# The work behind the ramp as single steps, put in order per engine by a list scheduler in the source

## The chip, the core and the metric

The kernel runs on one core of a Trainium2 chip. A core has five engines with instruction queues of their own: PE (matrix products into PSUM), DVE (vector work), ACT (activations, copies, casts), POOL (vector work on SBUF only) and SP (here it only issues DMAs). Each engine takes its instructions strictly in the order in which the program lists them; semaphores make an instruction wait for results of other engines, and whatever stands behind it on the same engine waits too. PE writes to PSUM, of which this kernel uses eight banks. The metric is the device time of the program in microseconds (us). It is 724.07 us before the change, the median of three runs (723.14 to 725.74).

## The reference

The first half is retention attention over blocks of 64 positions with a decay per head, the second a gated feed-forward network on its normed output. Cut to what matters:

```python
for b in range(nb):                               # per head, 12 blocks
    intra = (q[b] @ k[b].T) * Dmask               # decayed scores in the block
    out[b] = intra @ v[b] + (q[b] * lam_pow) @ kv_state
    kv_state = lam_block * kv_state + (k[b] * rev_pow).T @ v[b]
x = out.transpose(...).reshape(3072, 512)         # tokens x model
xn = x / sqrt(mean(x * x, -1) + 1e-6) * rms_g
y = (silu(xn @ w_gate) * (xn @ w_val)) @ w_out    # 512 -> 1536 -> 512
```

## The kernel before

The 3072 tokens are six *groups* of 512 (`m`, 0 to 5), the 1536 hidden columns twelve *column blocks* of 128 (`f`, 0 to 11). One group times one column block is a *unit*: the gate and val products, the silu of the gate, the hidden product, and four output products that add to four PSUM accumulators (`acc`, tags po0 to po3). There are 72 units: group 0 blocks 0 to 5, group 1 all twelve, group 0 blocks 6 to 11, and then groups 2 to 5. Every operand of a product is split into a high and a low part, so that each product is three.

Attention of a group runs in four *pairs* of heads (class `Pair`). A pair is: `scores` (PE), decays on ACT, DVE and POOL, `state_sums` (PE) and `states` (DVE), `mix_chunks` and `mix_states` (PE), then `keep_output` and `keep_squares` (ACT) and `add_squares`. Group m + 1 is worked on during group m. Its norm (class `Norm`) then takes: the squares split in two (`split_squares`), one row-sum product, a first guess and three refinements of the inverse root on DVE (`seed`, `refine`: three steps each on 128x512), four scalings (`scaled_to`), sums of the scaled parts, and their splits (`high` on ACT, `low` on DVE, `low_sums` on POOL).

There are three stretches.

- **The ramp** (`ramp`, units 0 to 5): written out by hand, with the first groups' attention and the first weights. The change leaves it alone.
- **Ordinary units** (6 to 23): `unit` issues gate (twelve matmuls, bank `pg`), val (twelve, bank `pv`), the hidden product `mul` (L958), `high` (L969) and `low` (L976), and the output products of the unit before. In between stand the conversion of the remaining weights (`Weights.take`, `split`), column norms and scale factors for the later half-precision weights (`columns`, `column_norms`, `bounds`, `factors`; the last two are some twenty small DVE steps), pairs of group 2 (units 16 to 20), whose `pst` and `po` use the banks `pg` and `pv`, its norm (21 to 23), the halving of the output weights (`halve_o`), and the weight sums (`WeightSums`).
- **Units of seven products** (24 to 71): `unit_of_sums` computes gate and val by seven products of half the width (Winograd's form of Strassen's scheme), six matmuls of 128x256 each, from sums of weights and sums of inputs. Two banks a and b take turns: products 1, 6, 7, 4 go to a and 2, 5, 3 to b; `keep` (ACT, L933) copies a aside, `sum` (DVE, L936) adds b to the copy, `silu_half` (L940) and `mul_sums` (L945) follow. In odd units a and b are the tiles `pg` and `pv`; in even units they are the two halves of one tile, `pp` (L919), which attention's scores and the norm also use. PE's order is written out: 1, 2, something to fill, 6, filler, 5, 7, filler, 4, filler, 3. The fillers are the output products of the unit before last (`outs`) and the pieces of attention. Refinement and scaling of the norm are queued with a cost each (`Tasks`) and drawn at two places of a unit.

The weight sums of block f (`WeightSums`: two adds on POOL, four sums on DVE, three casts on ACT, three remainders on POOL) are needed by the products of block f. `SUMS` puts them at units 18, 19, 20 and 24 to 32, and `HALVE` the halvings at units 18 to 20 and 24 to 26. `unit` issues a unit's DVE sums first (L1346), ahead of that unit's own `mul` (L1368).

What sets the order is the order of the calls alone: the source runs under a manual schedule, and waits are derived per tile from the calls as they were issued.

## Time and profile before

| | us |
|---|---|
| median of the runs (3) | 724.07 |
| the profiled execution | 722.93 |
| its span, first to last instruction | 721.1 |
| mean granted clock of PE over the span | 0.981 |

The span leaves out what lies before the first and behind the last instruction, 1.8 us. All work runs on one core, so the end of the chain is the end of the run. "Busy" of PE counts the time in which at least one matmul is under way; a matmul lasts longer than the distance to the next, so they overlap. Idle time shown in brackets is that of the engine just before the instruction, with what ended it. The names of tiles are those of the program: `pp`, `pa`, `pb`, `pg`, `pv` are banks of gate and val, `po`, `pst`, `pa` with L479 those of attention, `tx` stands for the sums of inputs and for the copies and sums beside them, `ws` and `r` for weight sums, `hh` for the hidden values.

### The profile page before, as it was taken

How to read it: one execution, taken by the hardware profiler on the slowest of the kernel's cores; microseconds unless marked ns; L12 is line 12 of the kernel's file. 1: busy time of each engine (PE TensorE's matmuls, PEld its weight loads, DVE VectorE, ACT ScalarE, POOL GpSimd, SP SyncE). 2: the span in 40 equal slices, each digit the busy share in tenths (PEclk: the TensorE clock that was granted, in tenths of full speed). 3: DMA queues.
4: the chain of work that ended last, by engine and by line, in shares of the span. 5: the costliest groups of instructions: out<-in, count | busy, mean ns of one | idle time of the engine just before them, and what ended most of it. 6: DMA issues, size and time to landing. Idle time of an engine off the chain costs nothing.

```text
span 721.1 us, 12347 instructions
## 1 busy us (share of the span) xinstructions
PE 662.8 (92%) x5007; PEld 444.3 (62%) x5007; DVE 423.2 (59%) x799; ACT 329.1 (46%) x674; POOL 158.4 (22%) x144
## 2 busy tenths in 40 slices
PE   8999999999977788789978899998899998899997
PEld 8755755555643445566656676666577666666664
DVE  6899667776544585566666443376543467533333
ACT  4795557775254424444424443334443334433332
POOL 3101110011265415577621111001111000000000
PEclk9999999999999998999989999999999999999999
DMA  8956423430130002201100131100130000010001
GB/s 322 354 202 234 175 89 108 155 117 0 60 117 1 1 0 73 71 34 60 59 1 1 59 118 59 59 2 1 59 117 2 1 2 1 4 56 1 1 0 60
DMA packets 14313, 51.13 MB, mean 71 GB/s; under 512 B 1712, under 2 KB 1968, under 8 KB 12848
## 3 DMA queue, kind: packets, MB, share of 16 engines
q1 hardware_dynamic: 13968, 49.69, 19.3%
q8 instruction: 39, 0.64, 0.4%
q10 hardware_dynamic: 288, 0.66, 0.3%
q14 instruction: 18, 0.15, 0.1%
HBM read 44.05 MB, written 6.29 MB: 70 GB/s over the span
## 4 chain that ended last, share of the span: by engine, by line
PE 44%; DVE 9%; ACT 6%; POOL 3%; issue 2%; DVEq 0%; ACTq 0%
PE pp L890 14%; PE pa L890 7%; PE pb L890 5%; PE acc L758 5%; PE acc L759 4%; PE acc L760 4%; DVE tx L936 2%; ACT sg L940 2%; PE po L539 2%; POOL r L829 1%; DVE sg L945 1%; ACT tx L933 1%; PE pa L479 1%; PE po L550 1%; DVE ws L840 1%
## 5 line engine op out<-in xcount | busy, mean ns | idle before, releaser
L759 PE MATMUL acc<-wo,hh 128*128 128x512 f16 (+1 forms) x288 | 111.4, 387 | 0.0
L760 PE MATMUL acc<-wo,hh 128*128 128x512 f16 (+1 forms) x288 | 111.3, 386 | 0.0
L758 PE MATMUL acc<-wo,hh 128*128 128x512 f16 x216 | 83.3, 386 | 0.2 <-DVE hh L976 0.2
L890 PEld LDWEIGHTS <-wg 128*128 128x128 f16 x576 | 56.2, 98 | 42.7 <-issue 23.3
L890 PEld LDWEIGHTS <-wo 128*128 128x128 f16 x576 | 55.8, 98 | 38.3 <-issue 16.5
L933 ACT COPY tx<-pp 128x256 f32<-128x256 f32 x72 | 26.8, 372 | 108.6 <-PE pp L890 107.8
L739 PE MATMUL pv<-x,wv 128*128 128x512 f16 x288 | 68.5, 386 | 5.0 <-ACT sq L582 5.0
L739 PE MATMUL pg<-x,wg 128*128 128x512 f16 x288 | 68.6, 383 | 0.3 <-ACT x L688 0.3
L969 ACT CAST hh<-sg 128x512 f16<-128x512 f32 (+1 forms) x72 | 44.6, 619 | 53.0 <-DVE sg L958 35.4
L890 PEld LDWEIGHTS <-wv 128*128 128x128 f16 x576 | 57.4, 100 | 17.0 <-issue 9.2
L933 ACT COPY tx<-pa 128x256 f32<-128x256 f32 x72 | 26.8, 372 | 84.6 <-PE pa L890 84.6
L499 POOL TENSOR_TENSOR qkv<-qkv,pw 128x512 f32<-128x512 f32 x22 | 29.2, 1330 | 127.7 <-PE pa L479 122.6
L936 DVE TENSOR_TENSOR tx<-pp,tx 128x256 f32<-128x256 f32 x48 | 20.4, 424 | 62.7 <-PE pp L890 51.0
L890 PE MATMUL pp<-x,wg 128*128 128x256 f16 x288 | 39.8, 275 | 15.5 <-ACT sg L940 12.9
L739 PEld LDWEIGHTS <-wv 128*128 128x128 f16 x288 | 27.9, 99 | 40.0 <-issue 8.9
L890 PE MATMUL pp<-tx,wo 128*128 128x256 f16 x288 | 40.0, 275 | 11.6 <-DVE tx L936 11.6
L739 PEld LDWEIGHTS <-wg 128*128 128x128 f16 x288 | 26.6, 98 | 34.3 <-issue 5.4
L890 PE MATMUL pp<-x,wv 128*128 128x256 f16 x288 | 37.5, 278 | 9.5 <-ACT x L688 6.9
L976 DVE TENSOR_TENSOR hh<-sg,hh 128x512 f16<-128x512 f32 x54 | 39.5, 731 | 9.3 <-ACT hh L969 7.7
L945 DVE SCALAR_TENSOR_TENSOR sg<-tx,cv,sg 128x512 f32<-128x512 f32 x48 | 39.1, 815 | 5.2 <-ACT sg L940 2.2
L940 ACT ACTIVATE sg<-sg,cg 128x256 f32<-128x256 f32 x48 | 24.4, 509 | 36.8 <-DVE sg L936 36.8
L936 DVE TENSOR_TENSOR tx<-pb,tx 128x256 f32<-128x256 f32 x48 | 20.4, 424 | 32.3 <-PE pb L890 29.5
(189 smaller groups left out, 1230.4 us busy)
## 6 DMA issues: line engine op xcount, KB each, us to landing
qkv<-in_qkv_dram SPq DMA_DIRECT2D x47, 512.0 KB, 4.9
raw_gv<-in_weights_dram SPq DMA_DIRECT2D x11, 1024.0 KB, 6.6
raw_o<-in_weights_dram SPq DMA_DIRECT2D x12, 512.0 KB, 3.9
out_dram<-o SPq DMA_DIRECT2D x23, 256.0 KB, 2.1
partial<-in_weights_dram SPq DMA_DIRECT2D x2, 512.0 KB, 11.7
qkv<-in_qkv_dram ACTq DMA_DIRECT2D x1, 512.0 KB, 4.5
out_dram<-o SPq DMA_DIRECT2D x1, 128.0 KB, 2.1
out_dram<-o ACTq DMA_DIRECT2D x1, 128.0 KB, 1.9
```

Source lines behind the costliest of these rows:

```text
L499: eng.tensor_mul(self.qT, self.qT, pw[:, p : p + 1, :].broadcast_to([P, GC, P]))
L739: nc.tensor.matmul(ps, w[:, kk, :], x[:, kk, :], start=i == kk == 0, stop=i == 2 and kk == NK - 1,)
L758: nc.tensor.matmul(acc, hl[:, ts_], oh, start=first, stop=False)
L759: nc.tensor.matmul(acc, hh[:, ts_], ol, start=False, stop=False)
L760: nc.tensor.matmul(acc, hh[:, ts_], oh, start=False, stop=last)
L890: nc.tensor.matmul(ps, w(ow, k), x(ox, k), start=first and i == k == 0, stop=i == 2 and k == 1, skip_group_check=True,)
L933: nc.scalar.copy(self.kept[:, i], self.pa)
L936: nc.vector.tensor_add(out, self.pb, self.kept[:, i])
L940: nc.scalar.activation(self.sg[:, half], src, AF.Silu, scale=cg[:, self.f, 0:1])
L945: nc.vector.scalar_tensor_tensor(self.sg, self.val, cv[:, self.f : self.f + 1], self.sg, ALU.mult, ALU.mult)
L969: nc.scalar.copy(self.hh, self.sg)
L976: nc.vector.tensor_sub(self.hl, self.sg, hh)
```

## The change

`unit`, `unit_of_sums`, `Tasks` and their helpers go. Their work becomes a list of steps. Each has an engine, a cost in us, a place `at` counted in units, the things it reads and writes by name, and the buffers that it opens. `Plan.run` goes through a model of the engines: it starts a step when what it needs is done, plus 0.15 us (0.28 from PE to ACT or DVE) and when a buffer is free. Of the steps up to 1.3 units ahead, PE takes the one with the smallest `at` that is ready; the other engines take the smallest `at`, or a later one that fits in ahead of it with at most 0.2 us lost. The step with the earliest start is then issued, so the program's order is the order of modelled starts. A DVE step that starts while POOL is at work costs a quarter more in the model. Loads (LD, LO) and stores (ST) are engines of the model; all go to SP's queue.

Other differences:

- Helpers are cut into single steps: `halve_o` becomes `Halves`, `columns` becomes `Column`, `scores`, `states` and `mix_chunks` go by two chunks each, `WeightSums` by parts. The two remainder buffers of a halving come from `o` (three buffers, shared with the output tiles) and no longer from `raw_o`.
- Groups 2 and 3 (`QUICK`) get the norm of the ramp: row sums with one column, the power -0.5 on POOL for 128x4 values, and a spread by four products (`quick`, `mean`, `root`, `spread`); the split of squares, the guess and the nine refinement steps go for these two groups. Groups 4 and 5 keep them.
- Weight sums are placed at 18.6, 19.6, 20.3 and from 24.5 on one per unit; halvings at 18.35 to 22.35 for blocks 6 to 11 and at 24.5 to 28.5 for blocks 0 to 5.
- The copy out of the accumulators and the store are steps of their own (`out_rows`, `send`).

```diff
@@ -691,7 +719,10 @@
             eng.tensor_sub(self.xl[:, kk, :], self.xns.pop(kk), self.xh[:, kk, :])
 
         def scaled_to(self, kk):
-
+            if self.m in QUICK and kk == 0:
+                r = self.r
...
+
+        def first(self, u):
+            self.banks(u)
+            self.add(1)
+
+        def add(self, n):
+            Product(self.m, self.f).add(
+                n, self.pb if n in (2, 5, 3) else self.pa, n in (1, 2, 5)
+            )
...
+        def sum_val(self, t, i):
+            half = slice(t * HG, (t + 1) * HG)
+            nc.vector.tensor_add(self.val[:, half], self.pb, self.kept[:, i])
+
+        def sum_gate(self):
+            self.sg = tmp.tile([P, G], F32, tag="t", name=f"sg_{self.m}_{self.f}")
+            nc.vector.tensor_add(self.sg[:, HG:], self.pb, self.kept[:, 0])
...
+    class Plan:
+
+
+        LAG = {("PE", "PE"): 0.0, ("PE", "ACT"): 0.28, ("PE", "DVE"): 0.28}
+        ENGINES = ("PE", "ACT", "DVE", "POOL", "LD", "LO", "ST")
 
...
+        def add(self, eng, cost, at, fn, *args, r=(), w=(), new=(), lasts=0.0):
+            self.steps.append((eng, cost, at, fn, args, tuple(r), tuple(w), tuple(new), lasts))
+
...
+        def run(self, horizon=1.3, reach=420):
+            deps = self.links()
...
+                best = None
+                for eng, c in found.items():
+                    now = clock[eng]
+                    c = sorted(x for x in c if x[1] < 1e9)
+                    if not c:
+                        continue
+                    pick = None
+                    if eng == "PE":
+                        pick = next((x for x in c if x[1] <= now + 0.05), None)
+                        pick = pick or min(c, key=lambda x: x[1])
+                    else:
+                        limit = 1e9
+                        for x in c:
+                            start = max(now, x[1])
+                            if start + self.steps[x[2]][1] <= limit + 0.2:
+                                pick = x
+                                if x[1] <= now + 0.05:
+                                    break
+                            limit = min(limit, start)
+                    start = max(now, pick[1])
+                    if best is None or start < best[0]:
+                        best = start, eng, pick[2]
...
+                start, eng, i = best
+                _, cost, at, fn, args, r, w, new, lasts = self.steps[i]
+                if eng == "DVE" and start < pool_until:
+                    cost *= 1.25
+                if eng == "POOL":
+                    pool_until = start + cost
+                clock[eng] = start + cost
+                end[i] = start + cost + lasts
+                if eng == "PE":
+                    progress = max(progress, at)
...
+                order.append((start, cost, eng, at, fn, args))
+                left.remove(i)
                 fn(*args)
...
+    def halve_steps(f, at):
+        h = Halves(f)
+        place = {HALF: NF, 0: NF - 1}.get(f, f - 1)
+        step("ACT", 0.72, at, h.high, r=["ts", "cv"], w=[f"w16_{f}:o", f"wo_{f}"], new=[(f"w16_{f}", f"wo{place}")])
+        step("ACT", 0.72, at + 0.1, h.rest_low, r=[f"wo_{f}", "ts"], w=[f"rl{f}", f"rh{f}"],
+             new=[(f"rl{f}", "o"), (f"rh{f}", "o")])
+        step("DVE", 0.76, at + 0.1, h.rest_high, r=[f"wo_{f}", "ts", f"w16_{f}:o"], w=[f"rh{f}"])
+        step("POOL", 1.28, at + 0.2, h.low, r=[f"rl{f}", f"rh{f}"], w=[f"w16_{f}:o"])
...
+    def sum_steps(f, at):
+        s = WeightSums(f)
+        tag = "w" if f < 3 else "a"
...
+            step("POOL", 1.15, at + 0.1 * i, s.whole, i, tag, r=[f"w{'vg'[i]}{f}"], w=[f"r{f}:{i}"],
+                 new=[] if i else [(f"r{f}", tag)])
+        for i in range(2):
+            step("DVE", 0.84, at + 0.5 + 0.1 * i, s.sums, i, to, r=[f"r{f}:0", f"r{f}:1"], w=[f"ws{f}"],
+                 new=[] if i else [(f"ws{f}", to)])
+        places = (
+            [f"w16_{ORDER[f]}:s"], [f"third{f}", "cols" if f < HALF else "partial"], [f"wg{f}"]
+        )
+        costs = [(0.6, 1.15), (0.4, 0.67), (0.4, 0.67)]
+        for i, to in enumerate(places):
+            step("ACT", costs[i][0], at + 0.9 + 0.05 * i, s.high, i, r=[f"ws{f}"], w=to)
+            step("POOL", costs[i][1], at + 1.2 + 0.05 * i, s.low, i, r=[f"ws{f}"], w=to)
...
+    def out_steps(u, h, ats):
+        m, f = h.m, h.f
+        first = f == 0 or (m == 0 and f == HALF)
+        weights = f"w16_{f}:o" if h.half else f"wo_{f}"
+        for t, at in enumerate(ats):
+            r = [f"hh{u}", weights] + ([] if h.half else [f"hl{u}"])
+            step("PE", 0.65 if h.half else 0.7, at, h.out, t, r=r, w=[f"acc{m}_{t}"],
...
+    def pair_scores(q, at):
+        n = f"{q.m}_{q.p}"
+        for i in range(2):
+            step("PE", 0.6, at + 0.02 * i, q.scores, range(2 * i, 2 * i + 2), r=[f"q{n}:q", f"q{n}:K"],
+                 w=[f"pa{n}"], new=[] if i else [(f"pa{n}", "ps")])
+        for j in range(2):
+            step("ACT", 0.5, at + 0.1, q.decay_k, j, w=[f"q{n}:k"])
+        step("DVE", 1.22, at - 1, q.decay_a, r=[f"pa{n}"], w=[f"a{n}"], new=[(f"a{n}", "a")])
+        step("POOL", 1.3, at + 0.1, q.decay_q, w=[f"q{n}:q"])
...
+    def pair_mix(q, at):
+        n = f"{q.m}_{q.p}"
+        m, p = q.m, q.p
+        for i in range(2):
+            step("PE", 0.54, at + 0.01 * i, q.mix_chunks, range(2 * i, 2 * i + 2), r=[f"q{n}:v", f"a{n}"],
+                 w=[f"po{n}"],
+                 new=[] if i else [(f"po{n}", "pv")] + [(f"x{m}", f"xs{SLOT_OF[m]}")] * (p == 0))
+        step("PE", 0.87, at + 0.05, q.mix_states, r=[f"q{n}:q", f"state{p}"], w=[f"po{n}"])
+        step("ACT", 0.57, at - 1, q.keep_output, r=[f"po{n}"], w=[f"x{m}:h{p}", f"x{m}:l{p}"])
+        step("ACT", 0.59, at - 1, q.keep_squares, r=[f"po{n}"], w=[f"s{n}"],
+             new=[(f"s{n}", "t" if p else "sq")])
...
+        if m in QUICK:
+            root = f"pr{m}"
+            step("PE", 0.9, at + 0.1, quick, r=[f"s{m}_0"], w=[f"pss{m}"], new=[(f"pss{m}", "ps")])
+            step("DVE", 0.25, at - 1, n("mean"), r=[f"pss{m}"], w=[f"y{m}"])
+            step("POOL", 1.0, at - 1, n("root"), w=[f"y{m}"])
+            step("PE", 1.0, at + 0.2, n("spread"), r=[f"y{m}"], w=[root], new=[(root, "ps")])
+            at -= 1
...
+    def strassen(u, h):
+        m, f = h.m, h.f
+        a, b = f"pa{u}", f"pb{u}"
+        banks = [(a, "pg"), (b, "pv")]
...
+        g, v = f"wg{f}", f"wv{f}"
+        s12, s3 = f"w16_{ORDER[f]}:s", f"third{f}"
+        step("PE", cost, u, h.first, u, r=[v, *x01], w=[a], new=banks)
+        step("ACT", 0.37, u - 1, h.keep, 0, r=[a], w=["kept0:0"])
+        step("PE", cost, u + 0.05, h.add, 2, r=[v, *x23], w=[b])
+        step("DVE", 0.42, u - 1, h.sum_val, 0, 0, r=[b, "kept0:0"], w=["kept1:0"])
+        step("PE", cost, u + 0.25, h.add, 6, r=[s12, *t], w=[a])
+        step("ACT", 0.37, u - 1, h.keep, 1, r=[a], w=["kept0:1"])
+        step("PE", cost, u + 0.4, h.add, 5, r=[s12, *t], w=[b])
+        step("PE", cost, u + 0.45, h.add, 7, r=[s3, *t], w=[a])
+        step("ACT", 0.37, u - 1, h.keep, 0, r=[a], w=["kept0:0"])
+        step("DVE", 0.42, u - 1, h.sum_gate, r=[b, "kept0:0"], w=[f"sg{u}:1"], new=[(f"sg{u}", "t")])
+        step("ACT", 0.47, u - 1, h.silu_half, 1, r=[f"cg{f}"], w=[f"sg{u}:1"])
+        step("PE", cost, u + 0.75, h.add, 4, r=[g, *x01], w=[a])
+        step("ACT", 0.47, u - 1, h.silu_half, 0, r=[a, f"cg{f}", f"sg{u}:1"], w=[f"sg{u}:0"])
+        step("PE", cost, u + 0.8, h.add, 3, r=[g, *x23], w=[b])
+        step("DVE", 0.42, u - 1, h.sum_val, 1, 1, r=[b, "kept0:1"], w=["kept1:1"])
+        step("DVE", 0.78, u - 0.9, h.mul_sums, r=["kept1:0", "kept1:1", "cv"], w=[f"sg{u}:0", f"sg{u}:1"])
+        tag = ("hh", "hl")[f % 2]
+        both = [f"sg{u}:0", f"sg{u}:1"]
+        step("ACT", 0.62, u + 0.2, h.high, r=both, w=[f"hh{u}"], new=[(f"hh{u}", tag)])
+        step("DVE", 0.7, u + 0.3, h.low, r=both, w=[f"hh{u}"])
+
...
+    QUICK = (2, 3)
+    SUMS = [(18, 18.6), (19, 19.6), (20, 20.3)]
+    SUMS += [(2 * NF, 2 * NF + 0.5 + 1.0 * (f - 3)) for f in range(3, NF)]
...
+            if HALF <= u - 1 < 2 * NF:
+                late = 0.66 if u < 2 * NF else 0.2
+                out_steps(u - 1, hs[u - 1], [u + late + 0.03 * t for t in range(GC)])
+            if 2 * NF <= u - 2:
+                out_steps(u - 2, hs[u - 2], [u + t for t in (0.15, 0.35, 0.6, 0.65)])
+            if u >= end:
                 continue
-            h = Hidden(m, f)
-
...
+                for i, f in enumerate(ORDER):
+                    halve_steps(f, u + 0.35 + 0.8 * i if i < HALF else 2 * NF + 0.5 + 0.8 * f)
+            for f, v in enumerate(SUMS):
+                if v[0] == u:
+                    sum_steps(f, v[1])
```

822 lines of the change are left out of this document (466 added, 356 removed).

## The prediction

> **What bounds the kernel now.** I read the page first, then the busy time by stage, then the waits of PE, then the timeline of a few units.
>
> ```profile
> span 721.1 us, 12347 instructions
> ...
> PE 662.8 (92%) x5007; PEld 444.3 (62%) x5007; DVE 423.2 (59%) x799; ACT 329.1 (46%) x674; POOL 158.4 (22%) x144
> ```
>
> PE is busy 92% of the span and no other engine is above 59%. So the kernel is bound by PE, and the change can only win where PE stands still, or runs on a lower clock. The stages show where that is. I cut at unit 7 (97.81), at 200, at the first unit of seven products (unit 24, 268.33), and at the first units of groups 3, 4 and 5 (395.06, 506.62, 616.90).
>
> ```profile
> core 0: us, PE busy (x) PEld busy (x) DVE busy (x) ACT busy (x) POOL busy (x), PEclk, DMA share, GB/s
> 97.81:200.00 102.19, 102.19 (x589) 59.69 (x589) 72.11 (x147) 59.03 (x107) 14.95 (x17) 1.00 0.27 93
> 200.00:268.33 68.33, 56.70 (x334) 28.84 (x333) 35.92 (x61) 28.78 (x52) 31.26 (x28) 0.93 0.09 31
> 268.33:300.00 31.67, 22.95 (x189) 16.51 (x189) 21.29 (x40) 14.09 (x31) 18.80 (x16) 0.87 0.20 68
> 300.00:395.06 95.06, 85.95 (x679) 59.64 (x675) 60.33 (x108) 41.28 (x96) 47.04 (x42) 0.96 0.10 34
> 395.06:506.62 111.56, 103.24 (x876) 74.21 (x874) 58.40 (x110) 44.42 (x98) 13.76 (x10) 1.00 0.14 48
> 506.62:616.90 110.28, 102.97 (x876) 74.12 (x874) 58.07 (x106) 43.72 (x97) 11.39 (x8) 1.00 0.09 30
> 616.90:721.10 104.20, 93.65 (x674) 65.50 (x671) 39.41 (x70) 36.28 (x79) 1.64 (x1) 1.00 0.06 21
> ```
>
> Length less PE's busy time is PE's idle time: 0, 11.6, 8.7, 9.1, 8.3, 7.3 and 10.5 us, together 55.6. Up to 200 PE never stops at full clock; there the change can only lose. Between 200 and 395 the clock is below 1, which costs at most (1 - clock) x busy: 4.0 + 3.0 + 3.4 = 10.4 us.
>
> ```profile
> engine line waited for: us in total, times, longest us
> PE pp L890 <- ACT sg L940: 12.9, 16, 1.7
> PE pp L890 <- DVE tx L936: 11.6, 23, 1.5
> PE pp L890 <- ACT x L688: 6.9, 2, 3.5
> PE po L539 <- DVE sg L958: 5.9, 2, 3.7
> PE pv L739 <- ACT sq L582: 5.0, 3, 2.3
> ```
>
> Each row gives a total, a count and the longest. These waits come from the order of the instructions, not from a lack of engine time. In an ordinary unit with attention, `po` and `pv` take turns in one bank:
>
> ```profile
> 218.54 1.09 PE L539 MATMUL po<-a,qkv 128*64 128x128 f32 x16 [3.69 <-DVE sg L958]
> ```
>
> ```profile
> 215.10 1.47 DVE L840 TENSOR_TENSOR ws<-r 128x256 f32<-128x256 f32 x1 [7.19 <-POOL r L829]
> ...
> 217.74 0.74 DVE L958 SCALAR_TENSOR_TENSOR sg<-pv,cv,sg 128x512 f32<-128x512 f32 x1
> ```
>
> PE waits 3.69 us for the hidden product (L958) that frees the bank. DVE stood still for 7.19 us before it, in front of a weight sum that waits for POOL, and the hidden product was queued behind that sum. On PE the four output products of the previous unit are queued behind the waiting matmul. The waits on L688 are the norm of the next group, which arrives late at two starts of a group. The first two rows of the waits are mostly the even units:
>
> ```profile
> 664.71 1.47 PE L890 MATMUL pp<-x,wv 128*128 128x256 f16 x12
> ...
> 666.28 0.37 ACT L933 COPY tx<-pp 128x256 f32<-128x256 f32 x1 [1.55 <-PE pp L890]
> ...
> 666.68 0.42 DVE L936 TENSOR_TENSOR tx<-pp,tx 128x256 f32<-128x256 f32 x1 [0.49 <-ACT tx L933]
> 667.16 0.82 PE L890 MATMUL pp<-tx,wo 128*128 128x256 f16 x6 [0.33 <-DVE tx L936]
> ...
> 671.06 0.82 PE L890 MATMUL pp<-x,wg 128*128 128x256 f16 x6
> ...
> 671.92 0.47 ACT L940 ACTIVATE sg<-pp,cg 128x256 f32<-128x256 f32 x1 [0.52 <-PE pp L890]
> 672.44 0.81 PE L890 MATMUL pp<-x,wg 128*128 128x256 f16 x6 [0.56 <-ACT sg L940]
> ...
> 673.09 0.82 PE L890 MATMUL pa<-x,wv 128*128 128x256 f16 x6
> ...
> 673.75 0.82 PE L890 MATMUL pb<-x,wv 128*128 128x256 f16 x6
> ...
> 674.00 0.38 ACT L933 COPY tx<-pa 128x256 f32<-128x256 f32 x1 [1.61 <-PE pa L890]
> ```
>
> In an odd unit (673.09) the two banks are two tiles, `pa` and `pb`, and the first copy (674.00) starts 0.25 after product 2 has begun, when product 1 is through. In an even unit both banks are one tile, `pp`: the copy at 666.28 waits for product 2 although it reads only what product 1 wrote, product 6 at 667.16 waits for a DVE sum of the other bank, and product 3 at 672.44 for the silu of the other bank. So what is issued earlier against either half of `pp` holds back what comes later. Each such stop costs its idle time and about 0.17 more, because the matmuls overlap: the six at 671.06 stand 1.38 us ahead of the next six, where 0.66 does without a stop (673.09 to 673.75), so the stop is worth 0.72 and shows 0.56 idle.
>
> **The change part by part.** (a) *Group 5, units 60 to 71* (10.5 idle). Six even units lose 0.33 + 0.56, together 5.3. Product 3 is now placed right behind product 4, ahead of the silu in program order, so the 0.56 goes; the silu then waits for product 3 too, some 0.65 later, and two products of the next unit cover that. The 0.33 stays: the plan names the halves of `pp` as separate things and puts the sum ahead of product 6, so the false wait survives. The longest wait for the DVE sum, 1.5 in the waits above, is in unit 60, behind the last norm's steps; 1.2 of it goes. The rest is the tail: the chain sum, product, cast, remainder, last outputs and stores, which no order shortens.
>
> ```profile
> 714.42 0.39 PE L758 MATMUL acc<-wo,hh 128*128 128x512 f16 x1 [0.16 <-DVE hh L976]
> ```
>
> PE waits only 0.16 there; the 6.7 us from this row to the end of the span hold the last twelve matmuls, then copies and stores. Nothing is won there. Saved: 3.4 + 1.2 and 7 times 0.17, 5.8 us.
>
> (b) *Groups 3 and 4* (15.6 idle). The same stops in 12 even units, and norm steps of the next group that stand ahead of the sums and silus. In the eight even units with attention the state sums now come in addition to the output product ahead of product 6, and fill the 0.33. DVE is busy half the time (58.4 of 111.6), so single norm steps fit into its holes two units earlier. I leave 4.5 idle and add 4 for some 24 starts: 15 us saved.
>
> (c) *Group 2, 268 to 395* (17.8 idle, clock 6.4 at most, of which I take 5, and 4 for some 24 starts: 27). The new short chain removes nine refinement steps and two before them:
>
> ```profile
> L675 DVE SCALAR_TENSOR_TENSOR hy<-yt,hy 128x512 f32<-128x512 f32 x12 | 8.3, 691 | 0.3
> ...
> L671 DVE TENSOR_TENSOR yt<-hy 128x512 f32<-128x512 f32 x12 | 8.3, 690 | 0.3
> ```
>
> ```profile
> L637 PE MATMUL pr<-ident,y x16: 273/275/356, 26.0 to 86.2; 128*128 128x128 f32 x16
> L628 POOL TENSOR_TENSOR y<-ms,power x2: 1023/1025/1027, 24.5 to 83.1; 128x4 f32<-128x4 f32 x2
> ```
>
> That is 9 x 0.69 = 6.2 us of DVE less for each of groups 2 and 3, and one POOL power of 1.03 and eight small fp32 matmuls more. On PE these cost at most 8 x 0.275 = 2.2 us a group, if none overlaps the next, and no less than 0, since the row sums that go are fewer; attention's products of the same width overlap (sixteen in 1.09 at 218.54), so I take half, 1.1, and 2.2 for both groups. The weight sums move to one per unit from unit 24.5 and all six later halvings come there too:
>
> ```profile
> L829 POOL TENSOR_TENSOR r<-wv 128x512 f32<-128x512 f16 x12 | 17.4, 1453 | 1.1 <-DMA out_dram<-o 1.1
> ...
> L268 POOL TENSOR_TENSOR wo<-rest 128x512 f16<-128x512 f32 x12 | 15.8, 1316 | 18.2 <-DVE rest L265 18.2
> L829 POOL TENSOR_TENSOR r<-wg 128x512 f32<-128x512 f16 x12 | 15.2, 1268 | 0.0
> ...
> L857 POOL TENSOR_TENSOR wo<-ws,wo 128x512 f16<-128x512 f32 x12 | 13.9, 1160 | 31.9 <-ACT wo L852 28.9 <-DVE hy L663 3.0
> ```
>
> (The first two columns after the bar are the total and the mean, in ns, of one.) One weight sum takes 2.7 for the two adds, 1.2 for the widest remainder, and two of half its width, which I put at 0.8 (between 0.6 and 1.2): 5.5 us of POOL, where the plan reckons 4.8. With 66 us now in these 127 and three halvings more (4 us), POOL would be busy 70 of about 105 us: two thirds, with 2.5 units of lead before a sum is used. DVE falls from 81.6 to about 75 of 105. Both fit, but both are in strict order, so a late POOL result stops everything behind its reader on DVE, the sums that free PE's banks among it. The halvings also leave `raw_o` for two of the three `o` buffers, which group 0's last output tiles hold until they are stored; there a halving can wait for a store, and a POOL addition behind it. I leave 10 of the 27: 17 saved.
>
> (d) *Units 18 to 23, from 200* (11.6 idle, clock 4.0 of which I take 3, 1.4 for starts: 16). The hidden product is given a unit's lead over the halvings and weight sums that now stand before it on DVE, and output products fill PE's waits for a bank. The chain bounds, spread, factors of unit 18 stays on the path of its product; attention and the output, gate and val products lie beside it. Where that cover fails, the price is the 3.69 seen above. I leave 5: 11 saved.
>
> (e) Units 6 to 17: same order of gate, val, output. Nothing to win; 1 us lost somewhere is my estimate between 0 and 4. Stores and loads still share SP's queue; a store that waits for its copy holds loads back, but those are due units later and DMA is at most 0.27 busy: nothing. Cutting a helper into single steps, and scores, states and mixes into halves, adds no instruction: nothing.
>
> Sum: 5.8 + 15 + 17 + 11 - 2.2 - 1 = 45.6. The profiled execution took 722.93 us (1.8 around its span), the median of runs 724.07, 1.1 more. 722.93 - 45.6 + 1.1 = 678.4; I say **678**.
>
> The ends: with every stop closed but the tail I get 657, with (c) and (d) at nothing 706; both are worked out next.
>
> **Rivals.** *The heavy stages give nothing back* (c and d fail, a and b hold): 20.8 - 3.2 = 17.6, **706**. For it speaks that between 200 and 395 DVE and POOL feed each other all the time; against it, that neither is above two thirds busy on average.
>
> *Slower.* The order is fixed by reckoned times, to 0.1 us, without slack. Its weak place is DVE beside POOL:
>
> ```profile
> L945 DVE SCALAR_TENSOR_TENSOR sg<-tx,cv,sg x48: 750/752/1753, 286.1 to 712.2; 128x512 f32<-128x512 f32 x48
> ```
>
> ```profile
> L840 DVE TENSOR_TENSOR ws<-r x12: 409/426/1484, 192.1 to 362.3; 128x256 f32<-128x256 f32 x12
> ```
>
> One block lasts about 1.0 us (1753 - 752; 1484 - 426), where the plan adds a quarter, 0.2. If one such block reached PE in each of the 48 last units, 48 us would eat the gain of 45.6; from there the kernel is slower, and with 60 blocks it is **738**. Against it: the medians sit at the minimum, and after 395 POOL works only 27 us in all. The Trainium skill, in "SBUF — State Buffer", section "SBUF: two separate sides", states that the port pair which DVE and GpSimd share is an exclusive lock held for a whole instruction; the longest rows agree, the medians say that it is rarely met. As an estimate by that page: if each of group 2's twelve hidden products lost one block of 1.0, the sum would be 33.6 and the time 690.
>
> *Everything closes*: all idle but 4 of tail, 8 of clock and 9 of starts, less 2: 67, **657**. *Nothing changes*, because the old waits return elsewhere one for one: 724.
>
> **How the numbers follow.** Forecast (662 to 697) 0.66; heavy stages fail (697 to 718) 0.16; all closes (under 662) 0.06; no change 0.03; slower 0.09. What a measurement can tell is about 0.3%, 2.2 us, so: faster 0.88, same 0.03, slower 0.09. The range leaves out the outer part of each side: 658 to 708.
>
> **What would show it.** PE's waits for the silu before product 3 gone, about 0.33 before product 6 left in even units without attention; clock 1.00 between 200 and 395; no wait on the casts of the norm at a group's start; PE without idle time up to 200. Wrong would be: PE waiting in group 2 on DVE sums that stand behind a weight sum or a halving, or DVE rows well over 0.75 us.

## The result, and the profile after

The changed kernel takes 671.0 us (median of four runs, 670.44 to 672.56), the kernel before 724.85 us beside it (723.14 to 725.74). The ratio is 0.9263, with a 95% interval of 0.9238 to 0.9288: 53.9 us less, where 46 were forecast. The profiled run of the changed kernel took 672.56 us, the longest of the four.

First the page of the changed kernel: the span, the busy time by engine, and PE's granted clock in forty slices (in tenths, so 9 stands for 90% or more).

```profile
span 670.8 us, 12331 instructions
...
PE 652.3 (97%) x5035; PEld 442.9 (66%) x5035; DVE 428.0 (64%) x779; ACT 328.9 (49%) x672; POOL 160.1 (24%) x144
...
PEclk9999999999999999999999999999999999999999
```

PE is busy 97% of the span. Its busy time fell by 10.5 us although 28 more of its matmuls are on record: the mean granted clock went from 0.981 to 0.998, and 0.017 of 662.8 us is 11.3, of the same size. DVE has 20 instructions fewer and is busy 4.8 us longer. That is taken up at the end.

Then the busy time by stage, in the order PE, PEld, DVE, ACT, POOL, with the granted clock behind them. The cuts are the first products of units 7, 18, 24, 36, 48 and 60.

```profile
100.26:195.68 95.42, 95.42 (x513) 54.49 (x512) 63.98 (x129) 56.13 (x102) 14.37 (x16) 1.00 0.25 85
195.68:258.65 62.97, 62.09 (x422) 33.38 (x422) 45.77 (x71) 30.60 (x55) 35.28 (x29) 1.00 0.15 50
258.65:366.76 108.11, 101.70 (x874) 73.80 (x873) 85.80 (x139) 57.34 (x129) 67.06 (x58) 1.00 0.15 50
366.76:473.34 106.58, 105.93 (x916) 76.42 (x914) 59.49 (x109) 45.98 (x101) 12.59 (x9) 1.00 0.15 51
473.34:573.89 100.55, 99.89 (x847) 72.92 (x846) 56.40 (x105) 42.26 (x92) 11.22 (x8) 1.00 0.09 32
573.89:670.80 96.91, 90.15 (x661) 64.34 (x659) 37.42 (x68) 34.88 (x77) 0.00 (x0) 0.99 0.06 23
```

Length less busy time of PE is its idle time: 0, 0.9, 6.4, 0.7, 0.7 and 6.8 us, together 15.4 where it was 55.6. The last 6.8 are 4.4 behind the last matmul and eight short stops. What is left to win sits in units 24 to 35, with 6.4. Set against the same units before (from first product to first product; the first row begins with unit 6, at 92.61 before and 94.36 now):

| units | before, us | after, us | won | forecast |
|---|---|---|---|---|
| 6 to 17 | 99.24 | 101.32 | -2.1 | -1 |
| 18 to 23 | 76.48 | 62.97 | 13.5 | 11 - 1.1 |
| 24 to 35 (group 2) | 126.73 | 108.11 | 18.6 | 17 - 1.1 |
| 36 to 59 (groups 3, 4) | 221.84 | 207.13 | 14.7 | 15 |
| 60 to the end | 104.25 | 96.89 | 7.4 | 5.8 |
| sum | | | 52.1 | 45.6 |

The spans differ by 50.3, not 52.1, because the ramp's first gate product starts at 33.87 us in this profile and at 32.10 in that of before. The ramp is the same code in both.

The waits of PE after (engine, line, what it waited for: total in us, times, longest):

```profile
PE pp L939 <- DVE tx L990: 3.1, 10, 0.3
PE pp L939 <- DVE sg L994: 2.6, 5, 0.7
PE pp L939 <- ACT tx L986: 2.2, 4, 1.0
...
PE pp L939 <- DVE xn L731: 0.9, 1, 0.9
```

The rows of 12.9 (silu), 11.6 (sums), 6.9 (casts of the norm), 5.9 (`po`) and 5.0 (`pv`) are gone. What heads the list is 3.1 us in ten stops of a third of a microsecond. They are the even units. The timeline of unit 70, PE first, then DVE, shows one:

```profile
645.89 1.47 PE L939 MATMUL pp<-x,wv 128*128 128x256 f16 x12
...
648.34 0.81 PE L939 MATMUL pp<-tx,wo 128*128 128x256 f16 x6 [0.33 <-DVE tx L990]
...
652.24 1.47 PE L939 MATMUL pp<-x,wg 128*128 128x256 f16 x12
```

```profile
647.86 0.42 DVE L990 TENSOR_TENSOR tx<-pp,tx 128x256 f32<-128x256 f32 x1 [0.49 <-ACT tx L986]
```

Products 4 and 3 now stand as one row of twelve at 652.24: the stop between them is gone. Product 6 at 648.34 still waits 0.33 us for a sum (647.86) that reads the other half of `pp`. Even units without attention went from 8.38 to 7.66 us, odd ones stayed at 7.17.

### The profile page after: what moved, and what is told of

Same layout as the page of the kernel before. It is cut to its first block, busy times and chain, and to the rows that moved or that the text cites. A ratio compares the mean times of both kernels' runs of the same rounds, so it can differ in the third digit from the quotient of the medians.

```text
span 670.8 us, 12331 instructions
## 1 busy us (share of the span) xinstructions
PE 652.3 (97%) x5035; PEld 442.9 (66%) x5035; DVE 428.0 (64%) x779; ACT 328.9 (49%) x672; POOL 160.1 (24%) x144
## 4 chain that ended last, share of the span: by engine, by line
PE 86%; DVE 8%; ACT 2%; POOL 1%; issue 1%; DMA 0%; DVEq 0%; ACTq 0%; POOLq 0%
PE pp L939 16%; PE pv L758 9%; PE acc L777 9%; PE pg L758 9%; PE pa L939 8%; PE acc L779 8%; PE acc L778 8%; PE pb L939 6%; PE pa L508 4%; PE po L569 3%; PE po L580 2%; PE pst L537 2%; DVE tx L990 1%; DVE ws L887 1%; ACT tx L986 1%
## 5 line engine op out<-in xcount | busy, mean ns | idle before, releaser
L758 PE MATMUL pv<-x,wv 128*128 128x512 f16 x288 | 67.0, 379 | 0.0
L990 DVE TENSOR_TENSOR tx<-pp,tx 128x256 f32<-128x256 f32 x48 | 20.3, 423 | 51.7 <-ACT sg L998 40.0
L1035 DVE TENSOR_TENSOR hh<-sg,hh 128x512 f16<-128x512 f32 x54 | 43.2, 800 | 5.1 <-ACT hh L1028 4.2
L1004 DVE SCALAR_TENSOR_TENSOR sg<-tx,cv,sg 128x512 f32<-128x512 f32 x48 | 39.6, 825 | 4.1 <-DVE tx L990 0.5
L994 DVE TENSOR_TENSOR sg<-pp,tx 128x256 f32<-128x256 f32 x24 | 10.1, 423 | 45.5 <-ACT tx L986 43.5
L939 PE MATMUL pp<-x,wg 128*128 128x256 f16 x288 | 35.5, 272 | 3.1 <-DVE sg L994 2.6
L990 DVE TENSOR_TENSOR tx<-pb,tx 128x256 f32<-128x256 f32 x48 | 20.3, 424 | 27.9 <-PE pb L939 25.1
L779 PEld LDWEIGHTS <-hh 128*128 128x128 f16 x216 | 21.1, 98 | 25.5
```

The lines of the kernel that those rows point to most:

```text
L758: nc.tensor.matmul(ps, w[:, kk, :], x[:, kk, :], start=i == kk == 0, stop=i == 2 and kk == NK - 1,)
L779: nc.tensor.matmul(acc, hh[:, ts_], oh, start=False, stop=last)
L939: nc.tensor.matmul(ps, w(ow, k), x(ox, k), start=first and i == k == 0, stop=i == 2 and k == 1, skip_group_check=True,)
L990: nc.vector.tensor_add(self.val[:, half], self.pb, self.kept[:, i])
L1004: nc.vector.scalar_tensor_tensor(self.sg, self.val, cv[:, self.f : self.f + 1], self.sg, ALU.mult, ALU.mult)
L1035: nc.vector.tensor_sub(self.hl, self.sg, hh)
```

## The experiments

All times are medians, with the ratio to the kernel before, run beside it, and its 95% interval. That kernel's own medians there lie between 723.64 and 724.93.

| run | what is in it | us | ratio [interval] |
|---|---|---|---|
| x1 | before, `pp` as two tiles | 701.94 | 0.9684 [0.9648, 0.9719] |
| x2 | after, two tiles | 666.09 | 0.9187 [0.9166, 0.9208] |
| x3 | after, no short chain | 687.54 | 0.9479 [0.9454, 0.9505] |
| x4 | after, short chain for group 2 alone | 672.86 | 0.929 [0.9265, 0.9314] |
| x5 | before, weight sums behind the hidden product | 723.88 | 0.9989 [0.9965, 1.0014] |
| x6 | x2, and the root copied out of PSUM | 666.47 | 0.9194 [0.9162, 0.9225] |
| x7 | after, planned without latencies | 695.78 | 0.9591 [0.9554, 0.9628] |
| x8 | x6, planned with POOL's costs as measured before | 667.58 | 0.9204 [0.9176, 0.9232] |
| x9 | x7 with two tiles | 663.45 | 0.9163 [0.9137, 0.9189] |
| x10 | before, short chain for group 2 | 728.42 | 1.007 [1.0042, 1.0098] |
| x11 | x9, short chain for group 2 alone | 662.75 | 0.915 [0.9108, 0.9191] |
| x12 | x9, no short chain | 670.86 | 0.9255 [0.922, 0.9289] |

### How much of the gain is the false wait

The prediction put some 0.5 to 0.9 us of every even unit on `pp`, one tile over two banks. Two tiles in place of one take these waits away with no change to the order.

```diff
-            self.pa = ps_att.tile([P, 2, GC, P], F32, tag="ps", name=f"pa_{m}_{p}")
+            self.pa = [
+                ps_att.tile([P, GC, P], F32, tag=g, name=f"{g}_{m}_{p}") for g in ("ps", "ps2")
+            ]
...
             if u % 2 == 0:
-                t = ps_att.tile([P, 2, G], F32, tag="ps", name=f"pp_{m}_{f}")
-                self.pa, self.pb = t[:, 0, :HG], t[:, 1, :HG]
+                self.pa = ps_att.tile([P, G], F32, tag="ps", name=f"pp_{m}_{f}")[:, :HG]
+                self.pb = ps_att.tile([P, G], F32, tag="ps2", name=f"pq_{m}_{f}")[:, :HG]
```

(The decay of the scores then takes two DVE steps of half the width, and the norm's single banks take one bank.) Put into the kernel before:

> The kernel before, with one edit: the two PSUM banks of the tag ps are two tiles, so that the banks a and b of an even unit are two tiles as in an odd one; attention's scores get one tile per head, and their decay is two DVE steps of 512 columns in place of one of 1024. Theory 'false waits' (a stop in an even unit comes only from both banks being one tile): twelve even units without attention give back 0.49 + 0.72 each, twelve with attention 0.49, together 20.5 us, so 704 to 707. Rival 'order' (DVE and ACT are simply late, because of what stands ahead of them): 722 to 726. The share of 20.5 that comes shows how much of the steady gain of the change could have been had without any new order.

It took 701.94 us, 22.6 less than before, and 2 us less than that theory's range. An even unit without attention, 66, on PE in this kernel, in its old order:

```profile
647.36 0.82 PE L895 MATMUL pp<-x,wv 128*128 128x256 f16 x6
648.01 0.82 PE L895 MATMUL pq<-x,wv 128*128 128x256 f16 x6
...
653.22 0.82 PE L895 MATMUL pp<-x,wg 128*128 128x256 f16 x6
653.88 0.82 PE L895 MATMUL pq<-x,wg 128*128 128x256 f16 x6
```

No row carries an idle time, and where two products follow each other they do so at 0.65 to 0.66 us. The unit takes 7.17 us (647.36 to the next unit at 654.53), as an odd one does. So two fifths of what the change brings can be had by naming the banks apart. Put into the changed kernel, where the plan gets the second name too:

> The changed kernel with the same edit of the tiles, in the source and in the plan's list of buffers. 'False waits': the 0.49 ahead of product 6 that is left in nine even units without attention goes (4.4 us), with a few stops of 0.4 to 0.6 in group 2: 664 to 667. Rival 'the plan leaves the 0.49 for another reason': 670 to 672.

666.09 us: the even units without attention drop to 7.17 as well. Two tiles are worth 22.6 us in the old order and 4.9 in the new one: by this reading the plan had won most of the false waits already, by putting products ahead of the reads.

### Whether the order hangs on the modelled times

The rival that ended slower said that the order is fixed by reckoned times without slack. The plan's only slack is the latency from engine to engine, the 0.2 us until a buffer counts as free, and the quarter for DVE beside POOL. All three are set to nothing:

```diff
-        LAG = {("PE", "PE"): 0.0, ("PE", "ACT"): 0.28, ("PE", "DVE"): 0.28}
+        LAG = {}
...
-                    t = max(t, end[d] + self.LAG.get((self.steps[d][0], eng), 0.15))
+                    t = max(t, end[d] + self.LAG.get((self.steps[d][0], eng), 0.0))
...
-                    t = max(t, sorted(free_at[tag])[k - 1] + 0.2)
+                    t = max(t, sorted(free_at[tag])[k - 1])
...
-                    cost *= 1.25
+                    cost *= 1.0
```

> The changed kernel, with a plan that knows no latency between engines (0 in place of 0.15 and 0.28), none for a buffer, and no extra cost of DVE beside POOL; the work is the same, only the order can differ. Theory 'the plan has no slack, so its model must be near': small stops all over, 680 to 695. Rival 'the priorities make the order, the model only breaks ties': 670 to 675.

695.78 us, 24.8 more than the changed kernel, just above the theory's range. By itself that reads as proof that the slack carries the order. The timeline of an even unit on PE says something else:

```profile
607.51 0.82 PE L939 MATMUL pp<-x,wv 128*128 128x256 f16 x6 [0.51 <-ACT tx L986]
...
614.19 0.82 PE L939 MATMUL pp<-x,wg 128*128 128x256 f16 x6 [0.56 <-ACT sg L998]
```

Products 2 and 3 wait for ACT's reads of the other half. Without latency the plan believes that a read starts the moment its product ends, issues it ahead of the next product, and the shared name turns that into a wait. Whether it is the name or the missing slack that costs 24.8 us, the same plan settings with two tiles decide.

> x7 and x2 together: no latency in the plan, and two tiles for the banks of the tag ps. If x7 lost its 25 us through the false waits (its longest wait is the silu ahead of product 3 in even units, 23 times, which the before kernel had too), two tiles give most of it back: 668 to 676. Rival 'an order without slack needs an exact model': the loss stays whatever the tiles are, 685 to 692.

663.45 us, 32.3 less than with one tile, better than either range, and no slower than x2 (the intervals overlap; behind the ramp the two profiles differ by 0.9 us). So the latencies mattered only because they happened to keep products ahead of reads that would have blocked them. Groups 3 and 4 in that kernel, by windows:

```profile
362.80:464.33 101.53, 101.53 (x877) 74.17 (x875) 57.85 (x110) 45.49 (x99) 13.72 (x9) 1.00 0.16 53
464.33:565.53 101.20, 101.20 (x876) 74.15 (x874) 57.30 (x108) 44.85 (x96) 11.99 (x8) 1.00 0.09 32
```

PE's busy time equals the length of both: it does not stop in 203 us. The rival's ground, an order without slack, does not hold in groups 3 and 4: what a semaphore delays there by a few tenths, the work that is queued on PE takes up.

### What the short norm chain is worth

```diff
-    QUICK = (2, 3)
+    QUICK = ()
```

> The changed kernel with the long norm chain for groups 2 and 3 too (no group is quick), order made by the same plan. My theory 'order is the gain': DVE has 14.6 us more to do and 2.2 us of small products leave PE; DVE is busy 64% of the span, so 671 to 677. Rival 'the short chain is the gain': the norm of groups 2 and 3 is late again, 3 to 4 us at the start of each group and more behind it, 680 to 690.

687.54 us: 16.5 more than the changed kernel, the rival's number. I had taken the order for nearly the whole gain, and that fell. Over units 18 to 47 (one cut apart, since work moves between the stages) it takes 292.56 us, the change 277.66, the kernel before 314.77. One stop of PE stands out, and DVE's timeline shows what it waits for:

```profile
263.87 1.08 PE L537 MATMUL pst<-qkv 128*64 128x64 f32 x16
273.52 1.12 PE L569 MATMUL po<-a,qkv 128*64 128x128 f32 x8 [8.56 <-DVE state L550]
274.57 2.74 PE L939 MATMUL pp<-x,wv 128*128 128x256 f16 x12
```

```profile
246.66 0.69 DVE L703 SCALAR_TENSOR_TENSOR hy<-yt,hy 128x512 f32<-128x512 f32 x1
...
265.38 0.75 DVE L816 SCALAR_TENSOR_TENSOR o<-acc,ik,partial 128x512 f32<-128x512 f32 x1
...
272.15 1.23 DVE L524 TENSOR_TENSOR a<-pa,mask 128x1024 f32<-128x1024 f32 x1
273.29 0.21 DVE L550 COPY state<-pst 128x64 f32<-128x64 f32 x1
```

The state sums of a pair of group 3 are ready at 264.95 (263.87 + 1.08), but the state step of 0.21 us starts at 273.29. DVE works with hardly a stop up to there: the last refinement of group 2 ends at 247.35, and its scalings and splits, outputs and weight sums stand ahead of the state. The steps are short; it is their place in one queue that costs 8.56. The clock falls with it: the twelve matmuls behind take 2.74 us at a granted clock of 0.50, where twelve such took 1.47 in unit 70. The short chain for group 2 alone:

> The changed kernel with the short chain for group 2 alone. Theory 'the short chain of group 3 holds the bank ps': the stops of about 5 us in units 31 and 32, where the spread inverse root sits in ps until four scalings have read it and product 1 of unit 32 waits for that, go, and 7 us of DVE work come back beside PE: 666 to 670. Rival 'DVE is too full in group 2': 673 to 678.

672.86 us, between the two ranges, with an interval that overlaps that of the change. So the 16.5 us are group 2's; the 1.9 that are left for group 3 can't be told from nothing. Group 3's long chain comes late in the same way, with a smaller stop, on PE:

```profile
371.32 0.69 PE L580 MATMUL po<-qkv,state 64*64 64x128 f32 x4 [1.57 <-DVE state L550]
```

Units 31 to 34 are shorter than in the change (together 30.89 us against 34.12), unit 35 is longer (21.17 against 10.11), most of it work that units 36 and 37 then lack (8.81 against 18.09): units 31 to 38 together take 73.31 against 72.03. Whether the short chain has a worth of its own was asked of the kernel before, with the root copied out of PSUM by ACT:

```diff
         if norm and step == NP + 1:
-            norm.row_sums()
-            norm.seed()
-            for _ in range(3):
-                norm.refine()
+            row_sums(norm.m, 0)
+            norm.mean()
+            norm.root()
+            norm.spread()
+            norm.root_out()
...
                 norm = Norm(2)
-                norm.split_squares()
```

> The kernel before with the short norm chain for group 2 alone, its root copied out of PSUM by ACT; nothing else. In the new order the short chain of group 2 was worth about 15 us (x3 against the changed kernel, less x4). If that worth hangs on the order (the chain is only late because the units before it became short): 719 to 724. Rival 'it is worth as much by itself': 708 to 712.

728.42 us, 4.8 *more* than before (1.0042 to 1.0098), where both theories expected a gain. On PE:

```profile
243.95 4.44 PE L747 MATMUL pv<-x,wv 128*128 128x512 f16 x12 [3.71 <-ACT sq L582]
...
251.85 2.07 PE L637 MATMUL pr<-ident,y 128*128 128x128 f32 x8 [2.67 <-POOL y L628]
```

Fewer DVE instructions, but four links PE, DVE, POOL, PE issued back to back, and PE stands 2.67 us at the last one with nothing put between. (The wait for the squares, 3.71, was 2.08 in the kernel before; why it grew was not followed.) In the changed kernel the plan puts the val product between the row sums and the spread, and the spread of group 2 starts without a stop:

```profile
233.25 1.05 PE L625 MATMUL pss<-ones,sq 128*128 128x1 f32 x8 [0.84 <-DVE sq L609]
234.17 2.75 PE L758 MATMUL pv<-x,wv 128*128 128x512 f16 x12
236.96 1.16 PE L658 MATMUL pr<-ident,y 128*128 128x128 f32 x8
```

The two last runs ask the same of the best order, x9:

> The same two-tile kernel planned without latencies (663.45), with no short chain at all. Theory 'the short chain is a term of its own, on DVE's queue, which two tiles do not touch': group 2's state step stands behind the refinements again, with one stop of about 8 us and long units 21 to 23, and the time is 16 us longer, 678 to 682. Rival 'the stop needed the false waits or the modelled latencies as well': less than half of it, 665 to 671.

> The two-tile kernel planned without latencies (663.45), with the short chain for group 2 only; group 3 gets the long chain back. Theory 'the long chain of group 3 comes too late in every order': its nine refinement steps push the state step behind the start of group 3, as before with the short chain for group 2 alone (unit 35 took 21 us, and the time was 1.9 us longer), so 664 to 667. Rival 'the stops of units 31 to 33 (11.74 and 8.49 us against 9.9 and 7.2) are the price of group 3's short chain and nothing else': they go, and the time is 659 to 662.

Without any short chain 670.86 us, 7.4 more than x9: the rival was right, less than half of the 16.5. The state step now comes in time (the one stop in units 18 to 23 is 0.84), and the price appears further on, where the weight sums of two blocks stand close together (that the norm's steps pushed them there is inferred). PE, then DVE, in units 27 and 28:

```profile
288.54 1.24 PE L510 MATMUL ps<-qkv 64*128 64x128 f32 x14 [2.66 <-DVE tx L995]
...
310.63 1.44 PE L944 MATMUL pq<-x,wg 128*128 128x256 f16 x6 [4.06 <-DVE sg L999]
```

```profile
302.14 1.37 DVE L891 TENSOR_TENSOR ws<-r 128x256 f32<-128x256 f32 x1
...
307.47 1.49 DVE L891 TENSOR_TENSOR ws<-r 128x256 f32<-128x256 f32 x1
308.88 1.37 DVE L892 TENSOR_TENSOR ws<-r 128x256 f32<-128x256 f32 x1
310.17 0.41 DVE L999 TENSOR_TENSOR sg<-pq,tx 128x256 f32<-128x256 f32 x1
```

The sum that frees PE's bank (310.17) stands behind weight sums that take 1.37 to 1.49 us, where one alone takes 0.42 (a row in the last section). POOL is at work beside them, from 299.77 to 305.93 and from 307.41 to 309.96, with no gap above 0.1 us in either stretch. That is the mechanism of the slower rival, with its price of about 1.0 each, in the place that the prediction named as its test. With the short chain for group 2 alone, 662.75 us is the lowest median of all, but within the scatter of x9: units 31 to 34 together shrink (33.03 to 30.73), unit 35 grows (8.37 to 11.33), and units 31 to 37 together take 58.98 against 59.48. The time lies between what the two theories expected. Group 3's short chain is worth nothing that can be measured, here as in the change.

### One step moved by hand

In the kernel before, the hidden product stood on DVE behind the weight sums. Here the sums alone move behind it.

```diff
     def unit(u, h, before, late, ready, wt, new, done, norm, step):
-        if u in SUMS:
-            SUMS[u].sums(u)
...
         h.low()
+        if u in SUMS:
+            SUMS[u].sums(u)
```

> The kernel before with one move: in an ordinary unit the four DVE sums of the weight sums stand behind that unit's hidden product and its remainder, no longer ahead of them. Theory 'queued behind a late weight sum': the 7.2 us that DVE stands in front of the sum in unit 19 no longer holds the hidden product, PE's wait of 3.7 and its like in unit 20 go: 715 to 719. Rival 'POOL is the path there': the weight sums come as late as before and the first units of seven products wait for them instead: 723 to 726.

723.88 us: no change, in the rival's range, though not by the rival's mechanism. Unit 19 falls from 21.07 to 17.11 us, units 20 and 21 rise from 13.85 and 11.96 to 16.12 and 14.72. PE's waits for `po` behind the hidden product are gone, and one row has grown from 5.0 to 11.8:

```profile
PE pv L739 <- ACT sq L582: 11.8, 3, 4.3
```

```profile
221.73 0.72 ACT L263 ACTIVATE wo<-wo,ts 128x512 f16<-128x512 f32 x1 [4.02 <-DVE rest L265]
...
225.91 0.60 ACT L852 CAST wo<-ws 128x512 f16<-128x512 f32 x1
...
227.50 0.59 ACT L582 ACTIVATE sq<-po 128x512 f32<-128x512 f32 x1
```

The squares that free the bank stand on ACT behind halvings and casts of the weight sums, and those now wait 4.02 us for DVE. The stop went from DVE's queue to ACT's. A gain needs the steps of a chain moved on all queues together, and that is what the plan does.

### Two guesses at the stops that are left in group 2

Between 318 and 360 us the changed kernel has eight stops, together 4.9 us, while group 3's norm is worked on. The longest:

```profile
337.14 1.49 PE L939 MATMUL pp<-x,wv 128*128 128x256 f16 x12 [0.88 <-DVE xn L731]
...
340.89 0.82 PE L939 MATMUL pp<-tx,partial 128*128 128x256 f16 x6 [0.99 <-ACT tx L986]
```

At 337.14 the bank itself is late: group 3's root stays in `ps`, the bank of even units, until four scalings (L731) have read it. Copied out at once by ACT, on top of x2:

```diff
+        def root_out(self):
+            pr = self.r
+            self.seed()
+            nc.scalar.copy(self.r, pr)
...
-            step("PE", 1.0, at + 0.2, n("spread"), r=[f"y{m}"], w=[root], new=[(root, "ps")])
+            step("PE", 1.0, at + 0.2, n("spread"), r=[f"y{m}"], w=[f"pr{m}"], new=[(f"pr{m}", "ps")])
+            step("ACT", 0.57, at - 1, n("root_out"), r=[f"pr{m}"], w=[root], new=rooms)
```

> The changed kernel with two tiles for the banks of the tag ps (as in x2) and, in groups 2 and 3, one copy by ACT that takes the spread inverse root out of PSUM, so that the bank is free after one reader and not after four scalings. Theory 'the short chain of group 3 holds the bank': the stops in units 31 to 33 go, 3 to 5 us less than x2, 661 to 664. Rival 'DVE and POOL are full there anyway': 665 to 668.

666.47 us, the same as x2: the rival. The wait for the scalings is gone, and the stops in that stretch come to 4.1 us against 3.4 in x2, with a new one for a hidden product's remainder:

```profile
PE acc L783 <- DVE hh L1041: 1.7, 2, 1.6
```

Then POOL's costs in the plan, as the trace of the kernel before has them:

```diff
-            step("POOL", 1.15, at + 0.1 * i, s.whole, i, tag, r=[f"w{'vg'[i]}{f}"], w=[f"r{f}:{i}"],
+            step("POOL", (1.45, 1.27)[i], at + 0.1 * i, s.whole, i, tag, r=[f"w{'vg'[i]}{f}"], w=[f"r{f}:{i}"],
...
-        costs = [(0.6, 1.15), (0.4, 0.67), (0.4, 0.67)]
+        costs = [(0.6, 1.16), (0.4, 0.82), (0.4, 0.80)]
```

> As x6, with the measured costs of POOL's weight sums in the plan (1.45 and 1.27 for the adds, 1.16, 0.82 and 0.80 for the remainders, in place of 1.15 and 1.15, 1.15, 0.67 and 0.67). If late POOL results stop DVE in group 2, the plan now sees it: 1 to 3 us less than x6. If not: within 1 us of x6.

667.58 us, no gain either, and the stops in that stretch come to 5.4 us. The costs were not those of this order: in x2 the two adds take 1.23 and 1.35 us and the widest remainder 1.24, so whether a plan with its own measured costs would do better stays open. The one version that keeps the short chain for group 3 and has little of these stops is x9, planned without latencies: 1.8 us in the same stretch, and 59.48 us for units 31 to 37 against 61.53 in x2. Which of its placings does that was not taken apart and stays open.

## Why the prediction came out as it did

**The bound.** That the kernel is bound by PE and can win only its 55.6 idle and the clock held: 40.2 of the idle went, and the clock is 1.00 in the five stages from 100.26 to 573.89.

**(a) Group 5.** The mechanism is right to the row: the silu wait ahead of product 3 gone, the 0.33 ahead of product 6 left. 7.4 came instead of 5.8, but 2.6 of it is work that moved across the stage's first cut: unit 59 has 24 output matmuls on record where it had 12, and takes 9.76 us where it took 7.17. Without that, 4.8 were won, 1.0 less than forecast; 0.4 of the 1.0 is unit 71 with the tail (17.23 us against 16.82). Such shifts change a row of the table and not the sum.

**(b) Groups 3 and 4.** 14.7 came, 15 forecast; with the 2.6 that moved into unit 59 it is 17.3. The same two stops are only a part of it: unit 36 won 4.5 us and units 47 to 49 won 3.8, where a group's norm had come late; the six other even units with attention won 0.64 each, together 3.8; and units 44, 46, 56 and 58 won 5.3. That the row came out so close is in part the moved work.

**(c) and (d) The heavy stages.** 32.1 came, 25.8 forecast (28 less 2.2). I left 10 and 5 us idle there; 6.4 and 0.9 are left. A sign that was to show the prediction wrong did appear, at a small size: in group 2, PE waits 0.60, 0.42 and 0.73 us (at 267.65, 283.71 and 321.22) for a sum (L994) that stands on DVE behind weight sums or a halving's remainder, 1.8 us in all. One of the three, PE and then DVE:

```profile
283.71 1.47 PE L939 MATMUL pp<-x,wg 128*128 128x256 f16 x12 [0.42 <-DVE sg L994]
```

```profile
281.83 1.49 DVE L887 TENSOR_TENSOR ws<-r 128x256 f32<-128x256 f32 x1
283.25 0.41 DVE L994 TENSOR_TENSOR sg<-pp,tx 128x256 f32<-128x256 f32 x1
```

These waits are part of the 6.4 that are left, so the 10 set aside covered them.

**The short chain** is the step that was mis-sized. The prediction priced it by what DVE is busy with, 6.2 us less per group, as relief inside (c), and put 2.2 against it. Measured, it is 16.5 us in the changed kernel (x3), 7.4 in the order of x9 (x12), and a loss of 4.8 in the old one (x10). A chain of dependent steps on a strict queue is priced by what is queued behind its last link, not by its busy time; and the fill between its links is the order's work. Without it, units 18 to 47 would have won 22.2 us instead of 37.1. That the sum came close owes something to this: the terms (c) and (d) were set by how much idle I left, without saying which part closes it.

**(e) Units 6 to 17.** -2.1, within the estimate of 0 to 4. It is not work moved across the cut: from unit 6 to unit 17 both traces have the same matmuls of each kind on record (132 output matmuls, for one). Unit 6 lost 0.7, with a stop of 0.54 at its end, and unit 16 lost 0.9, the other ten together 0.5. Between 100.26 and 195.68 PE has no idle time, so what made unit 16 longer is no stop, and stays open.

**The rivals.** Heavy stages giving nothing: not so. Nothing changes: not so, though x5 shows that it is what happens to a single moved step. Everything closes (657): x9 and x11 come within 7 of it, with two tiles and a plan without latencies. Slower through DVE beside POOL: the blocks came, mostly where the prediction did not count them. It counted them on the hidden product (L945, now L1004) and reckoned 48 to lose everything. The rows of the changed kernel (minimum, median, maximum in ns):

```profile
L1004 DVE SCALAR_TENSOR_TENSOR sg<-tx,cv,sg x48: 750/752/1925, 270.6 to 661.5; 128x512 f32<-128x512 f32 x48
```

The median stayed at 752. Ten of the 48 are more than 0.1 us longer than the shortest, where four were before. Over group 2's twelve the excess is 2.4 us, not the 12 of the estimate that gave 690. The second of a block's four weight sums, before (L841) and after (L887), shows more:

```profile
L841 DVE TENSOR_TENSOR ws<-r x12: 411/418/421, 192.4 to 362.6; 128x256 f32<-128x256 f32 x12
L887 DVE TENSOR_TENSOR ws<-r x12: 412/1372/1495, 196.0 to 354.0; 128x256 f32<-128x256 f32 x12
```

Over all four sums, 4 of 48 last more than 1.2 us before and 15 now. The four were all in the first sum, L840, the very row whose median the prediction read as "rarely met": it hid a third of the cases. PE does wait behind such sums: 0.42 us at 283.71 above, and 4.06 in x12, where several come together.

How the shares stand, on a path that the runs walk from the kernel before to x9: two tiles alone 22.6 (724.51 to 701.94), the order planned without latencies on top of them 31.1 (to x12's 670.86), the short chain on top of that 7.4 (to x9's 663.45), together 61.1. On another path the shares differ, since the order wins most of the false waits too. The change's own 53.9 were walked with one tile and a plan with latencies, and stop 7.6 short of x9.

## What to carry to other kernels

Where two banks take turns, give them two names before anything is reordered: each access to a shared name waits for the accesses to it that were issued earlier, and an order, planned or by hand, will then be tuned around waits that need not exist. Price a chain of small dependent steps by what stands behind its last link in each queue, and move all links together: one moved step sends the stop to the next queue, and a shorter chain without work between its links can lose. A planner's modelled latencies may matter for another reason than the one they stand for; take them out and look at the rows before tuning them.

## What the hardware showed that was not expected

DVE got busier with less to do: 428.0 us in 779 instructions against 423.2 in 799. The 48 weight sums take 36.8 us where they took 24.5, more than the whole difference. Two of them in the changed kernel, DVE and then POOL:

```profile
261.56 0.42 DVE L886 TENSOR_TENSOR ws<-r 128x256 f32<-128x256 f32 x1
261.90 1.50 DVE L887 TENSOR_TENSOR ws<-r 128x256 f32<-128x256 f32 x1
```

```profile
261.79 1.32 POOL L282 TENSOR_TENSOR wo<-rest_h,rest_l 128x512 f16<-128x512 f32 x1 [5.68 <-DVE rest_h L277]
```

The sum that began before POOL's add took 0.42; the one that began 0.11 behind its start took 1.50, and ended at 263.40, 0.29 behind the add's end at 263.11. The Trainium skill, in "SBUF — State Buffer", section "SBUF: two separate sides", says that whichever of DVE and GpSimd starts first holds their shared port pair for its whole instruction, a DVE step counting when both its inputs lie in SBUF, as here; these rows agree. A factor of 1.25 on DVE's cost, as in the plan, has the wrong shape for it: the row shows a wait for the rest of POOL's instruction, whatever DVE's own length.
